# Rows 4p+j in a block, wider load pieces, loads in waves and a first projection by parts in a fused attention and GLU kernel

## The chip, the cores and the metric

The kernel runs on one core of one Trainium2 chip. The time is device microseconds (us) of one execution. A profile's span starts with the first instruction; in these runs the time is about 1.8 us more than the span of the same execution. Comparisons below use the mean time of one kernel's fast runs over that of the other's fast runs of the same rounds, so a ratio is not quite the ratio of the medians quoted beside it. A run more than 1.5% above the fastest of its kernel is called slow and left out of the ratios; for a kernel whose runs scatter the ratio therefore flatters, and the slow runs are named.

## The reference, cut to what matters

```python
x = A_x                                        # 2048 x 512, bf16
h  = x + attention(layernorm(x)) @ wo          # 32 heads of 16, each position sees
                                               # 8 earlier ones, at distances 0, 2, .. 14
h2 = h + ((relu(n @ W_gate)) * (n @ W_up)) @ W_down    # n = layernorm(h), 1376 wide
```

q, k and v come from one 512 x 1536 weight. The attention looks back by position, so k and v must lie in the order of the sequence along a free dimension: the kernel keeps them transposed, features on partitions and positions along the row.

## The kernel before

Four blocks of 512 rows. Each block: statistics on VectorE (DVE), normalised rows, transposes to `xnT`, then twelve groups of four matmuls (q, k, v) whose result ScalarE (ACT) copies out of PSUM, the memory that TensorE (PE) writes to:

```python
x_rows = A_x.rearrange("b (tb p) d -> p (b tb) d", p=P)        # 1 KB pieces
...
for j in range(BPC):
    (nc.scalar if j % 2 else nc.sync).dma_start(x_sm[:, j:j + 1, :], x_rows[:, j:j + 1, :])
for c, q in enumerate((nc.sync, nc.scalar, nc.sync)):          # q, k, v weights
    q.dma_start(w3_sb[c][:], w3_r[:, :, c * D:(c + 1) * D])
for tk in range(1, NCK):                                       # the other blocks of x at once
    nc.sync.dma_start(x_sm[:, tk * BPC:(tk + 1) * BPC, :], x_rows[:, tk * BPC:(tk + 1) * BPC, :])
# ... all other weights ...

def f_mm(lo=0, hi=CS, ...):                                    # one q, k or v group
    for dt in range(NT):
        nc.tensor.matmul(mm.t[:, lo:hi], lhsT=w3_sb[c][:, dt, t:D:NT],
                         rhs=xnT.t[:, dt, lo:hi], start=(dt == 0), stop=(dt == NT - 1))

def f_ev(...):                                                 # its copy out of PSUM
    o = qT.t[:, t, :]            # or kT / vT[:, t, PADL + s0: PADL + s0 + CS]
    nc.scalar.copy(out=o, in_=mm.t[:])
```

The order of instructions on each engine is planned in the program from a table of ranks; the change brings a new table. Matmuls of 128 x 128 `warm` tiles at the start keep TensorE busy while nothing has landed.

The softmax here doesn't subtract the row's maximum and nothing guards it: scores larger than these inputs give would overflow.

## Time and profile before

| | before |
|---|---|
| time, median of the first 3 runs | 203.12 us (202.84 to 203.56) |
| span of the profiled execution | 203.6 us |
| PE busy | 195.4 us |
| ACT busy | 127.7 us |
| first real matmul starts | 10.13 us |

The prediction shows the lines that carry the bound. Two more views matter for what came: the row of the copies of q (those of k and v take the same), with columns count, busy us, mean ns of one, then idle time before and what ended it:

```profile
L519 ACT CAST quad<-bank 128x512 bf16<-128x512 f32 x16 | 9.6, 601 | 7.4 <-PE bank L511 7.4
```

and the table of stretches (start:end, length, busy PE, PEld (PE's weight loads), DVE, ACT, POOL (GpSimd), then granted clock, DMA share, GB/s):

```profile
15.00:20.00 5.00, 5.00 (x38) 3.77 (x36) 4.58 (x12) 3.63 (x9) 0.00 (x0) 0.94 1.03 404
20.00:30.00 10.00, 9.89 (x81) 4.84 (x80) 10.00 (x14) 8.01 (x14) 0.00 (x0) 1.00 0.56 188
30.00:84.00 54.00, 53.56 (x333) 25.64 (x336) 53.45 (x64) 43.75 (x88) 5.56 (x7) 1.00 0.33 64
...
13.70:68.50 54.80, 54.36 (x351) 28.54 (x356) 53.83 (x81) 43.93 (x87) 3.59 (x4) 0.98 0.47 129
```

See the ACT column: ScalarE is a "63%" engine over the whole span, but from 20 to 84 us it is busy 51.8 of 64. The last row runs from the first of the 48 copies to the end of the last: 43.9 of 54.8 us busy, only 10.9 idle.

### The profile page before, as it was taken

What the parts mean: (1) busy time and instruction counts of PE and PEld (TensorE: products, weight loads), DVE (VectorE), ACT (ScalarE), POOL (GpSimd) and SP (SyncE); (2) the same over time, 40 slices, a digit from 0 to 9 for tenths busy, and PEclk for the clock granted to TensorE, in tenths of its full rate; (3) what the DMA queues carried; (4) which work ended last, traced back from release to release, by engine and by line L of the source; (5) the groups of instructions that cost most, each with busy time, mean ns of one, the idle gap of its engine ahead of it and who ended that gap; (6) DMA issues with size and microseconds to landing.
All of it is one profiled execution on the core that took longest, in us unless ns stands there. A gap on an engine that the chain in (4) does not pass through costs nothing.

```text
span 203.6 us, 2957 instructions
## 1 busy us (share of the span) xinstructions
PE 195.4 (96%) x1102; PEld 96.8 (48%) x1123; DVE 155.1 (76%) x246; ACT 127.7 (63%) x253; POOL 12.6 (6%) x26
## 2 busy tenths in 40 slices
PE   8499999999999999999999999999999999999994
PEld 8347545555545334444454444444444445444452
DVE  6549999999999999999999966599996255021314
ACT  3517879986569993797756599703665353576400
POOL 3000000330000002400033000000000000000000
PEclk9859999999999999999999999999999999999999
DMA  5999901698000002980059900400011001100003
GB/s 187 350 379 403 322 19 30 123 203 163 3 0 0 0 3 52 192 168 0 3 103 180 209 31 0 90 13 0 3 41 62 0 0 53 53 0 0 0 3 103
DMA packets 14893, 18.04 MB, mean 89 GB/s; under 512 B 5056, under 2 KB 12192, under 8 KB 14880
## 3 DMA queue, kind: packets, MB, share of 16 engines
q1 hardware_dynamic: 12336, 10.78, 16.4%
q0 software_dynamic: 1728, 6.29, 16.3%
q10 hardware_dynamic: 816, 0.79, 1.1%
q8 instruction: 9, 0.15, 0.3%
q14 instruction: 4, 0.03, 0.0%
HBM read 8.42 MB, written 2.10 MB: 52 GB/s over the span
## 4 chain that ended last, share of the span: by engine, by line
PE 93%; DMA 4%; issue 1%; SPq 0%; DVE 0%
PE bank L736 38%; PE bank L511 22%; PE bank L773 19%; PE bank L698 7%; DMA wq_sb<-in_A_wqkv_dram 4%; PE bank L564 4%; PE bank L465 2%; PE bank L625 1%; PE bank L597 1%; SPq L270 0%; DVE row L784 0%
## 5 line engine op out<-in xcount | busy, mean ns | idle before, releaser
L736 PE MATMUL bank<-quad,wg_sb 128*128 128x512 bf16 (+1 forms) x171 | 42.3, 379 | 0.3
L736 PE MATMUL bank<-quad,wu_sb 128*128 128x512 bf16 (+1 forms) x173 | 42.3, 379 | 0.1
L743 ACT ACTIVATE gr<-bank 128x512 bf16<-128x512 f32 (+1 forms) x44 | 26.0, 604 | 23.7 <-PE bank L736 18.3
L773 PE MATMUL bank<-wd_sb,gT 128*128 128x512 bf16 (+3 forms) x184 | 39.7, 366 | 0.2
L558 DVE TENSOR_TENSOR big<-quad,kT 128x4096 bf16<-128x4096 bf16 x16 | 36.0, 2284 | 0.1
L646 DVE TENSOR_TENSOR big<-big,vT 128x4096 bf16<-128x4096 bf16 x16 | 35.8, 2283 | 0.3 <-ACT big L631 0.3
L740 ACT CAST up_sb<-bank 128x512 bf16<-128x512 f32 (+1 forms) x44 | 25.7, 594 | 12.3 <-PE bank L736 8.5
L756 DVE TENSOR_TENSOR gT<-gr,up_sb 128x1024 bf16<-128x1024 bf16 (+1 forms) x24 | 15.4, 643 | 20.4 <-ACT gr L743 14.1
L773 PEld LDWEIGHTS <-gT 128*128 128x128 bf16 (+1 forms) x187 | 18.0, 98 | 19.3 <-issue 0.4
L736 PEld LDWEIGHTS <-wu_sb 128*128 128x128 bf16 (+1 forms) x176 | 17.3, 100 | 20.7 <-issue 1.3
L736 PEld LDWEIGHTS <-wg_sb 128*128 128x128 bf16 (+1 forms) x176 | 17.3, 100 | 20.6 <-issue 1.1
L511 PE MATMUL bank<-quad,wq_sb 128*128 128x512 bf16 (+1 forms) x70 | 16.9, 382 | 2.5 <-DMA wq_sb<-in_A_wqkv_dram 2.1
L631 ACT CAST big<-bank 128x512 bf16<-128x512 f32 x32 | 17.2, 610 | 1.5 <-PE bank L625 1.3
L511 PE MATMUL bank<-quad,wk_sb 128*128 128x512 bf16 (+1 forms) x70 | 16.8, 373 | 0.1
L678 POOL DMA_DIRECT2D big<-big x12 | 10.7, 894 | 98.3 <-DVE big L646 95.2
L784 DVE TENSOR_TENSOR row<-x_sm,bank 128x512 bf16<-128x512 bf16 (+1 forms) x17 | 10.6, 652 | 7.8 <-PE bank L773 7.8
L649 DVE TENSOR_TENSOR big<-big 128x1024 bf16<-128x1024 bf16 (+2 forms) x24 | 16.4, 727 | 0.0
L709 DVE SCALAR_TENSOR_TENSOR x_sm<-x_sm,bank 128x512 bf16<-128x512 bf16 x16 | 10.9, 685 | 6.8 <-PE bank L698 6.7
L511 PE MATMUL bank<-quad,wv_sb 128*128 128x512 bf16 x62 | 15.4, 379 | 0.1
L698 PE MATMUL bank<-wo_sb,quad 128*128 128x512 bf16 x61 | 14.8, 379 | 0.2
L371 ACT ACTIVATE row<-x_sm,mv 128x512 bf16<-128x512 bf16 x16 | 11.5, 717 | 4.5 <-DVE mv L363 4.4
L519 ACT CAST quad<-bank 128x512 bf16<-128x512 f32 x16 | 9.6, 601 | 7.4 <-PE bank L511 7.4
(65 smaller groups left out, 161.7 us busy)
## 6 DMA issues: line engine op xcount, KB each, us to landing
big<-big POOLq DMA_DIRECT2D x12, 512.0 KB, 5.5
out_dram<-row SPq DMA_DIRECT2D x15, 128.0 KB, 1.7
x_sm<-in_A_x_dram SPq DMA_DIRECT2D x3, 512.0 KB, 11.0
wu_sb<-in_B_W_up_dram SPq DMA_DIRECT2D x1, 1376.0 KB, 10.6
wg_sb<-in_B_W_gate_dram SPq DMA_DIRECT2D x1, 1376.0 KB, 13.9
wd_sb<-in_B_W_down_dram SPq DMA_DIRECT2D x1, 1280.0 KB, 15.7
wq_sb<-in_A_wqkv_dram SPq DMA_DIRECT2D x1, 512.0 KB, 8.4
wk_sb<-in_A_wqkv_dram ACTq DMA_DIRECT2D x1, 512.0 KB, 8.6
```

Of the source, the lines that this page charges most:

```text
L371: nc.scalar.activation(out=xn.t[:], in_=h.t[:] if h else x_sm[:, tk * BPC + j, :], func=ACT.Square, bias=mv.t[:, j, 0:1], scale=1.0, accum ...
L511: nc.tensor.matmul(mm.t[:, lo:hi], lhsT=w3_sb[c][:, dt, t:D:NT], rhs=xnT.t[:, dt, lo:hi], start=(dt == 0), stop=(dt == NT - 1))
L558: V.tensor_tensor(out=pb.t[:].rearrange("p (t w) s -> p t w s", t=2), in0=q4, in1=k4, op=ALU.mult)
L631: nc.scalar.copy(out=ab.t[:, w, :], in_=bc.t[:])
L646: V.tensor_tensor(out=mt.t[:], in0=ab.t[:], in1=v8, op=ALU.mult)
L649: V.tensor_tensor(out=mt.t[:, 0:n, :], in0=mt.t[:, 0:n, :], in1=mt.t[:, n:2 * n, :], op=ALU.add)
L698: nc.tensor.matmul(od.t[:], lhsT=OT.t[:, t, j * P:(j + 1) * P], rhs=wo_sb[:, t, :], start=(t == 0), stop=(t == NT - 1 and tk not in RPE))
L736: nc.tensor.matmul(mm.t[:fs, :], lhsT=w_sb[:, dt, ft * P: ft * P + fs], rhs=hnT.t[:, dt, :], start=(dt == 0), stop=(dt == NT - 1))
L740: nc.scalar.copy(out=ub.t[:fs, i, :], in_=um.t[:fs, :])
L743: nc.scalar.activation(out=gr.t[:fs, i, :], in_=gm.t[:fs, :], func=ACT.Relu)
L756: V.tensor_tensor(out=gt.t[:fs, 0:n, :], in0=gr.t[:fs, 0:n, :], in1=ub.t[:fs, 0:n, :], op=ALU.mult)
L773: nc.tensor.matmul(od.t[:, c0:c1], lhsT=gts[ft].t[:fs, ft % 2, j * P:(j + 1) * P], rhs=wd_sb[:fs, ft, c0:c1], start=(ft == 0), stop=(ft == ...
```

## The change

The intent is to start TensorE earlier: x in 2 to 4 KB pieces and the q and k weights in 2 KB pieces, first what the first projection needs and the rest behind it, and the projection begun on 128 rows as soon as those are ready. Larger pieces of x need partition p to hold the rows 4p to 4p+3 of a block, so that transposed columns come out in the order (j, p) and the copies must put them back in the order of the sequence.

```diff
-    x_rows = A_x.rearrange("b (tb p) d -> p (b tb) d", p=P)
+    x_rows = A_x.rearrange("b (tk p j) d -> p (b tk) j d", p=P, j=BPC)     # output rows likewise
+        for j, q in ((0, nc.sync), (2, nc.scalar)):
+            q.dma_start(x_sm[:, j:j + 2, :], x_rows[:, 0, j:j + 2, :])
+        for dt in range(NT):                          # q and k together, 256 KB a time
+            (nc.scalar if dt % 2 else nc.sync).dma_start(wqk_sb[:, dt:dt + 1, :], w3_r[:, dt:dt + 1, 0:2 * D])
 ...
+        nc.gpsimd.tensor_copy(out=x_sm[0:1, BPC, 0:1], in_=x_sm[0:1, 0, 0:1])      # wait for x block 0
+        nc.sync.dma_start(x_sm[:, BPC:2 * BPC, :], x_rows[:, 1, :, :])
+        nc.gpsimd.tensor_copy(out=wv_sb[0:1, 0, 0:1], in_=wqk_sb[0:1, 3, 0:1])     # wait for q, k
+        nc.sync.dma_start(wv_sb[:], w3_r[:, :, 2 * D:3 * D])
 ...                                                   # then the other blocks and weights
-                nc.scalar.copy(out=o, in_=mm.t[:])
+                nc.scalar.copy(out=o.rearrange("p (c j) -> p j c", j=BPC),
+                               in_=mm.t[:].rearrange("p (j c) -> p j c", j=BPC))
 ...
-    nc.tensor.matmul(od.t[:], lhsT=OT.t[:, t, j * P:(j + 1) * P], rhs=wo_sb[:, t, :], ...)
+    nc.tensor.matmul(od.t[:], lhsT=OT.t[:, t, j:CS:BPC], rhs=wo_sb[:, t, :], ...)
```

Cut: block 0's fourth statistic moves from ScalarE to VectorE, the first four q/k groups go in parts of 128, 128 and 256 rows, filler matmuls follow the first transposes, 44 warm-up matmuls instead of 48, and the table of ranks is new and obeyed strictly.

## The prediction

> **What bounds the kernel now.** I read the page's busy shares and slices first, then the chain of waits in order of time, then the timeline of the first 20 us, then a table of stretches for the granted clock.
>
> ```profile
> PE 195.4 (96%) x1102; PEld 96.8 (48%) x1123; DVE 155.1 (76%) x246; ACT 127.7 (63%) x253; POOL 12.6 (6%) x26
> ...
> PE   8499999999999999999999999999999999999994
> ...
> DVE  6549999999999999999999966599996255021314
> ...
> PEclk9859999999999999999999999999999999999999
> DMA  5999901698000002980059900400011001100003
> ```
>
> See: a slice is 5.09 us. TensorE is full from the fourth slice to the last, so from about 15 us on nothing but the amount of matmul work can move the end. The only soft places are the first three slices, where PE is at 8 and 4 tenths and the granted clock at 8 and 5. DVE is also at 9 from the fourth slice to the twenty-first: a second engine without slack there.
>
> The chain in order of time says which wait ends last in the soft part:
>
> ```profile
> 1.61 0.05 issue
> 1.66 8.42 DMA wq_sb<-in_A_wqkv_dram
> 10.08 0.05 issue
> 10.13 2.32 PE bank L511 x9
> 12.45 0.22 issue
> 12.67 7.27 PE bank L511 x38
> ...
> 200.69 0.42 DVE row L784
> ```
>
> See: one 512 KB weight load, issued at 1.66 us, lands 8.42 us later; the first real matmul waits for it. After it the chain is PE without a break to 200.69. The tail (last add and store, 203.6 - 200.69 = 2.9 us) is untouched by the change.
>
> The timeline shows that the data side was ready before the weights:
>
> ```profile
> 3.48 1.29 DVE L401 BATCH_NORM_STATS2 st<-x_sm 128x6 f32<-128x512 bf16 x2 [0.29 <-DMA x_sm<-in_A_x_dram]
> ...
> 6.21 1.38 DVE L436 TENSOR_SCALAR row<-x_sm,mv,rs 128x512 bf16<-128x512 bf16 x4 [0.20 <-ACT rs L418]
> ...
> 7.51 0.75 DVE L477 COPY quad<-bank 128x512 bf16<-128x512 bf16 x2
> ...
> 10.13 2.32 PE L511 MATMUL bank<-quad,wq_sb 128*128 128x256 bf16 x9 [2.08 <-DMA wq_sb<-in_A_wqkv_dram]
> ```
>
> See: all of the first block's normalised rows are transposed and copied out by about 8.7 us (a ScalarE copy ends then); PE idles 8.05 to 10.13.
>
> The idle time has a second price, the clock:
>
> ```profile
> 8.00:9.00 1.00, 0.05 (x1) 0.00 (x0) 0.26 (x1) 0.61 (x2) 0.00 (x0) 0.90 0.96 310
> 9.00:10.00 1.00, 0.00 (x0) 0.00 (x0) 0.00 (x0) 0.00 (x0) 0.00 (x0) 0.50 1.09 382
> ...
> 14.00:15.00 1.00, 1.00 (x4) 0.40 (x3) 1.00 (x3) 0.35 (x1) 0.00 (x0) 0.50 1.03 401
> 15.00:16.00 1.00, 1.00 (x5) 0.38 (x3) 1.00 (x6) 0.53 (x1) 0.00 (x0) 0.69 1.05 402
> 16.00:17.00 1.00, 1.00 (x7) 0.51 (x5) 1.00 (x2) 0.56 (x3) 0.00 (x0) 1.00 1.01 392
> ```
>
> Columns: stretch, length, busy PE, PEld, DVE, ACT, POOL, then granted clock, DMA share, GB/s. The clock falls to half at about 8.8 (0.90 in that row) and returns at about 15.6. By 16.29 PE did eight 256-column and twelve 512-column matmuls, 8192 columns. At full clock 512 columns take 0.216 us (x38 pieces in the later chain; 1.73 us for x8), so these are 16 x 0.216 = 3.45 us of work that took 16.29 - 10.13 = 6.16. The half clock costs 2.7 us.
>
> **What the Trainium skill says.** "TensorE: Matmul & The Clock Gate", Part 1 (The HAM clock gate): the array's clock is halved by default and after an idle window, restored after a busy one; the window is 3.4 us and free-running. The trace agrees: 8.8 to 15.6 is 6.8 us, two windows. Free-running also means that its phase against the kernel differs by run, which fits the 0.7 us spread of three runs. "DMA: Bandwidth & Descriptors", Issuing engines are not separate DMA queues: loads from several queues interleave on the same 16 engines. Agrees: the DMA share is about 1.0 from 4 to 25 us, so wq waited for its competitors. The same page, Specifications, puts line rate at pieces of 512 B and more; here 1 KB pieces moved at about 350 GB/s (5 to 8 us) and the later mix, with 2.7 and 4 KB pieces among it, at about 400 (14 to 20 us). So I allow larger pieces 10 to 15%, no more. "SBUF — State Buffer", Door 1: lines of 16 bytes, two or more hits in one run at full rate; the new strides of 4 bf16 are 8 bytes. For reads the trace agrees: the strided q/k weight loads take 113 to 118 ns against 98 for contiguous ones, hidden behind 216 ns matmuls. No ScalarE write of this stride is in the trace.
>
> **The change part by part.**
> Larger pieces and waves. Before, x block 0, q, k, v (2 MB) and three more x blocks were all put on the queues by 4 us. Now only x block 0 and q/k (1.57 million bytes) go first, the rest waits behind tiny GpSimd copies that depend on the loads. Bytes start at about 1.9 us (33 GB/s in the row 1:2). At 350 to 380 GB/s they are through at 1.9 + 1.57/0.365 = 6.2, and with up to 1 us from last byte to the waiting engine wq/wk should be usable at about 7.0 instead of 10.08. x block 0 should be there at about 3.7 (3.48 for its first 128 KB row group before). x block 1 follows, 0.52 million bytes more, about 8.5.
> So the weights stop being the bound, and the chain of block 0's layernorm takes over. DVE now takes all four statistics (ScalarE took one), in this static order: two statistics 3.7 to 5.0, two aggregates to 5.3, the third statistic to 6.0, aggregate 6.1, the normalised rows at 6.2, 6.5 and 6.9 (0.33 apart; ScalarE's Ln and Exp of 0.3 and 0.2 before each), the fourth statistic to 7.9, two PSUM copies and an aggregate (0.34 + 0.15 + 0.34) to 8.7, one statistic of block 1 (0.65, if it has landed) to 9.4, the fourth row 9.8. Then a transpose, a ScalarE copy of 0.6: the last 256 rows can be projected from about 10.9 to 11.1.
> Meanwhile PE does 12 transposes, 16 filler matmuls (0.9 us in idle time), then 32 matmuls of 128 columns. Their pace is 56 ns by columns; weight loads of this stride might make it 70 to 113. At 70, 32 x 0.07 = 2.2 us, from 8.5 to 10.7: in time. The first four groups then need 16 matmuls of 256 columns (0.11 each, 1.8 us) and the other four 16 of 512 (3.45 us). The q/k projection of block 0 ends at 11.0 + 5.25 = 16.3, if the clock stays whole. Before, it ended at 19.78, with the same 16 transposes done.
> The rest. Matmul counts after that are the same; before took 203.6 - 19.78 = 183.8 us for it. Moved: strided ScalarE copies of q, k, v (48, about 0.6 us each, I leave them at that), strided loads of wo's stationary operand (hidden), a new fixed order. The first score matmuls need two DVE products of 2.28 us, after the evictions and, in the new order, three statistics of block 2 among them; I get them ready at about 20.9, where PE is ready at 16.3 + 0.9 + 3.45 = 20.7. I add 0.4 us for stalls there and at the second scores.
> Sum: 183.8 + 16.3 + 0.4 = 200.5 us, 1.3% below 203.12. Of the 3.5 us gained at the front 2.7 is clock and the rest earlier weights.
>
> **The rivals.** (1) The clock falls again anyway: warm-up ends at 5.5, the transposes come in three bursts from 6.6, and if the window's phase is bad PE is at half rate for part of the projection. For: before, a stretch that was 63% busy (8.85 to 12.27) did not bring the clock back. Against: fillers cover 7.6 to 8.5 and projection parts follow. It would give 201.5 to 203. (2) LayerNorm faster or weight parts quicker than I think, no stalls: 199 to 199.8. (3) DVE, saturated from 13 to 110 us, becomes the bound: PE's gain is then only DVE's, whose first product moves from 18.84 to about 15; or block 1's x lands late and holds DVE's strict order before the fourth row. 201 to 201.5. (4) Strided ScalarE writes run at half pace: 48 x 0.6 = 29 us more on an engine at 63%, first products 2 us later, 201.5 to 203. No row speaks for it.
>
> **Range and chances.** The middle case gets about 0.55, rivals 1, 3 and 4 together 0.3, rival 2 0.15. Predicted 200.5 us, 199.0 to 202.4 for 8 in 10. Faster by over 2% means below 199.06: 0.12. Within 2%: 0.85. Slower: 0.03; only a badly fitting fixed order could do that.
>
> **What would show it.** Right: wqk's wait gone from the chain or ending near 7 us; the 128-column parts beginning near 8.5, the 256-column ones near 11; clock 1.00 in every row from 8 to 17; the next transposes after the q/k projection near 16.3; ScalarE copies of k still about 600 ns; PE unbroken to the end. Wrong: a wait for wqk beyond 8, a clock of 0.5 after 8, copies near 1 us, PE idle before the score matmuls beyond 1 us.

## The result, and the profile after

| | before | after |
|---|---|---|
| time, median of 6 runs | 203.13 us (202.71 to 204.5) | 223.32 us (222.65 to 224.82) |
| ratio of fast runs | | 1.099 (95%: 1.0945 to 1.1036) |
| ACT busy | 127.7 us | 153.6 us |

10% slower, far outside the range. The page's first lines of the changed kernel (a slice is now 5.6 us):

```profile
PE 202.1 (91%) x1151; PEld 98.4 (44%) x1151; DVE 156.4 (70%) x247; ACT 153.6 (69%) x251; POOL 12.6 (6%) x28
...
PE   7798687957899849999999999999999999999993
...
ACT  2489999997999999668775666693145494157600
...
PEclk9999799999999995999999999999999999999999
```

PE has gaps up to the fifteenth slice, and ACT is at 9 over just this part. The chain of waits, merged in order of time, says the same:

```profile
12.52 0.20 ACT rs L438
12.73 1.20 ACT kT L535
13.93 1.16 ACT quad L535
15.09 1.16 ACT kT L535
16.24 1.16 ACT quad L535
17.40 2.31 ACT kT L535 x2
```

From 12.5 to 83.6 us nearly every link of it is a ScalarE instruction, mostly L535, the copy of q, k or v. Its row, to be held against L519 above:

```profile
L535 ACT CAST quad<-bank 128x512 bf16<-128x512 f32 x16 | 21.8, 1410 | 0.0
```

1410 ns where it was 601, and no idle time before any of them. Those of k and v take 1393 and 1412 ns: together 64.3 us busy for the 48 copies, where they had 28.5. (Neighbouring copies overlap in the records: a copy takes 1.41 us, but the next starts 1.15 us after it. So the sum of these rows is more than the time that they occupy, and the page's total for ACT rose less, from 127.7 to 153.6.) The stretches:

```profile
15.00:20.00 5.00, 5.00 (x37) 3.02 (x36) 3.26 (x3) 5.00 (x6) 0.00 (x0) 1.00 1.02 411
20.00:30.00 10.00, 6.51 (x36) 2.20 (x35) 7.19 (x9) 10.00 (x11) 0.00 (x0) 0.83 0.69 240
30.00:84.00 54.00, 43.08 (x256) 20.31 (x255) 41.21 (x59) 52.66 (x68) 3.59 (x4) 0.99 0.26 49
```

ACT is full, PE and DVE starve, and PE's gaps bring back a half clock now and then (0.83 in the second row). Yet the front is nearly as it was meant to be. The timeline there:

```profile
8.49 1.50 PE L526 MATMUL bank<-quad,wqk_sb 128*128 128x128 bf16 x24
...
9.07 0.70 DVE L421 BATCH_NORM_STATS2 st<-x_sm 128x6 f32<-128x512 bf16 x1 [0.45 <-DMA x_sm<-in_A_x_dram]
...
11.21 5.36 PE L526 MATMUL bank<-quad,wqk_sb 128*128 128x256 bf16 x32 [0.23 <-ACT quad L501]
...
14.82 1.42 ACT L535 CAST kT<-bank 128x512 bf16<-128x512 f32 x1
15.97 1.43 ACT L535 CAST quad<-bank 128x512 bf16<-128x512 f32 x1
```

The parts begin at 8.49, the last 256 rows at 11.21, and the first transposes of the next block follow the projection at 16.41. The copies start 1.15 us apart. One wait was not meant: x block 1 landed at 9.05 us, and DVE, held to its fixed order, waited 0.45 us for it before it could make the fourth row of block 0.

### The profile page after: what moved, and what is told of

The parts are those of the page before. It is cut to its first block, busy times and chain, and to the rows that moved or that the text cites. A ratio compares the mean times of both kernels' runs of the same rounds, so it can differ in the third digit from the quotient of the medians.

```text
span 223.0 us, 3021 instructions
## 1 busy us (share of the span) xinstructions
PE 202.1 (91%) x1151; PEld 98.4 (44%) x1151; DVE 156.4 (70%) x247; ACT 153.6 (69%) x251; POOL 12.6 (6%) x28
## 3 DMA queue, kind: packets, MB, share of 16 engines
q1 hardware_dynamic: 10800, 10.78, 14.7%
## 4 chain that ended last, share of the span: by engine, by line
PE 61%; ACT 30%; DMA 4%; DVE 2%; issue 1%; POOL 0%; ACTq 0%
PE bank L753 36%; PE bank L790 17%; ACT kT L535 8%; ACT quad L535 7%; ACT vT L535 7%; PE bank L715 5%; DMA x_sm<-in_A_x_dram 4%; ACT quad L501 2%; ACT big L648 2%; PE bank L581 1%; ACT row L410 1%; DVE big L575 1%; PE bank L642 1%; ACT ex L597 1%; DVE st L421 1%
## 5 line engine op out<-in xcount | busy, mean ns | idle before, releaser
L753 PE MATMUL bank<-quad,wg_sb 128*128 128x512 bf16 (+1 forms) x176 | 44.5, 391 | 2.8 <-ACT quad L501 2.8
L753 PE MATMUL bank<-quad,wu_sb 128*128 128x512 bf16 (+1 forms) x176 | 43.8, 385 | 0.0
L526 PE MATMUL bank<-quad,wqk_sb 128*128 128x512 bf16 (+2 forms) x160 | 31.7, 342 | 2.1 <-ACT kT L535 1.3
L526 PEld LDWEIGHTS <-wqk_sb 128*128 128x128 bf16 x160 | 15.9, 115 | 15.5 <-issue 6.7
L535 ACT CAST kT<-bank 128x512 bf16<-128x512 f32 x16 | 21.1, 1393 | 1.2 <-DVE big L575 1.2
L535 ACT CAST quad<-bank 128x512 bf16<-128x512 f32 x16 | 21.8, 1410 | 0.0
L535 ACT CAST vT<-bank 128x512 bf16<-128x512 f32 x16 | 21.4, 1412 | 0.0
L526 PE MATMUL bank<-quad,wv_sb 128*128 128x512 bf16 x64 | 17.0, 394 | 2.9 <-ACT vT L535 2.4
L666 DVE TENSOR_TENSOR big<-big 128x1024 bf16<-128x1024 bf16 (+2 forms) x24 | 17.3, 730 | 0.2
L501 ACT COPY quad<-bank 128x1024 bf16<-128x1024 bf16 (+1 forms) x12 | 11.2, 968 | 7.9 <-PE bank L485 7.9
```

Source lines behind the costliest of these rows:

```text
L501: nc.scalar.copy(out=o, in_=i)
L526: nc.tensor.matmul(mm.t[:, lo:hi], lhsT=wv_sb[:, dt, t:D:NT] if c == 2 else wqk_sb[:, dt, c * D + t:(c + 1) * D:NT], rhs=xnT.t[:, dt, lo:h ...
L535: nc.scalar.copy(out=o.rearrange("p (c j) -> p j c", j=BPC), in_=mm.t[:].rearrange("p (j c) -> p j c", j=BPC))
L666: V.tensor_tensor(out=mt.t[:, 0:n, :], in0=mt.t[:, 0:n, :], in1=mt.t[:, n:2 * n, :], op=ALU.add)
L753: nc.tensor.matmul(mm.t[:fs, :], lhsT=w_sb[:, dt, ft * P: ft * P + fs], rhs=hnT.t[:, dt, :], start=(dt == 0), stop=(dt == NT - 1))
```

## The experiments

Theory S: the store with a step of four bf16 elements (8 bytes) makes each copy more than twice as long, and this alone makes ScalarE the bound. Rivals: the new order or the waves (O); other traffic that slows the copies (C); any walk of more than one dimension or with a large step, on either side of the copy (R).

**The four that decide.** The first takes the step away and keeps everything else, the order too (its result is wrong):

```diff
-  nc.scalar.copy(out=o.rearrange("p (c j) -> p j c", j=BPC), in_=mm.t[:].rearrange("p (j c) -> p j c", j=BPC))
+  nc.scalar.copy(out=o, in_=mm.t[:])
```

> The changed kernel with one thing undone: the 48 copies of q, k and v out of PSUM write 512 neighbouring elements instead of every fourth (the result is wrong on purpose, rows land in the wrong order; the instruction order on every engine stays). Theory S (the store with a step of 8 bytes is what makes these copies 1.40 us long and ScalarE the bound from 12.6 to 83.6 us): the copies are back at about 0.60 us, ScalarE's busy time is about 38 us lower, PE is unbroken, and the time is 201 to 203 us. Rival O (the new fixed order or the waves of loads cost the time): the copies shorten but PE still has gaps before 84 us and the time stays above 212. Rival C (the copies are slow because of other traffic at that time): the copies stay above 1 us.

202.5 us median (202.44, 202.53 and 202.47, and a slow run of 207.26), ratio to before 0.992 (0.986 to 0.998). The profile, of 200.6 us span:

```profile
L535 ACT CAST quad<-bank 128x512 bf16<-128x512 f32 x16 | 9.3, 602 | 1.4 <-PE bank L526 1.3
```

```profile
30.00:84.00 54.00, 53.59 (x326) 25.90 (x330) 53.72 (x57) 41.84 (x83) 7.04 (x8) 1.00 0.41 77
```

The copies are short, PE is full again. The whole loss was in that one line; O and C fall. ACT's busy time is 123.4 us, 30.2 below the changed kernel and not the 38 expected: the 38 took the overlap of the copies for work. From the first copy to the end of the last, first the changed kernel, then this one:

```profile
12.50:86.50 74.00, 59.59 (x345) 27.99 (x344) 55.39 (x75) 72.63 (x86) 3.59 (x4) 0.95 0.38 110
...
12.20:65.50 53.30, 52.84 (x339) 27.19 (x344) 52.49 (x75) 42.43 (x86) 3.59 (x4) 1.00 0.52 149
```

The same 86 ScalarE instructions fill 72.6 of 74.0 us, and here 42.4 of 53.3. The step adds 30.2 us of work; idle time takes up 9.5 of it (10.9 us idle become 1.4), and the stretch is 20.7 us longer. With 0.3 us before it and 1.4 after it, that is the 22.4 us between the spans.

The second brings the natural order of rows back and keeps the waves, parts, fillers and order (a correct kernel):

```diff
-  x_rows = A_x.rearrange("b (tk p j) d -> p (b tk) j d", p=P, j=BPC)      # out_rows likewise
+  x_rows = A_x.rearrange("b (tk j p) d -> p (b tk) j d", p=P, j=BPC)
-  nc.scalar.copy(...)  with the step;   lhsT=OT.t[:, t, j:CS:BPC]
+  nc.scalar.copy(out=o, in_=mm.t[:]);   lhsT=OT.t[:, t, j * P:(j + 1) * P]
```

> The changed kernel with rows in their natural order again (x in 1 KB pieces, contiguous copies, contiguous stationary operand of wo), but waves, 2 KB pieces of the q and k weights, the parts of 128 rows, fillers and the new fixed order kept; a correct kernel. Theory S: as the plain-copy run, 201 to 203 us, within 1 us of it, because 2 or 4 KB pieces of x move the first statistic by 0.3 us at most. If the pieces of x matter, it is over 1 us slower than the plain-copy run. Rival O: above 212.

The profiled execution has a span of 201.2 us, 0.6 above the plain-copy one; its 256-column parts begin at 11.39, 0.4 later than there (10.97). The timed runs were 203.03 and 205.28, and two slow ones of 208.29 and 207.34: ratio 1.014 (1.005 to 1.023): unclear, for a reason that came out later. So the pieces of x, the price of which was the whole reordering, are worth at most about half a microsecond in these two profiles, and even that is not shown: the changed kernel, with the large pieces, began at 11.21. What differs is x block 1: it landed at 9.05 us there and at 9.23 here, and DVE waited for it; in the plain-copy profile it landed at 8.32, and DVE did not wait.

The third keeps the rows 4p+j and puts the same reordering on the read side of the copy (correct):

```diff
-  nc.scalar.copy(out=o.rearrange("p (c j) -> p j c", j=BPC), in_=mm.t[:].rearrange("p (j c) -> p j c", j=BPC))
+  nc.scalar.copy(out=o.rearrange("p (c j) -> p c j", j=BPC), in_=mm.t[:].rearrange("p (j c) -> p c j", j=BPC))
```

> The changed kernel with the same reordering done on the other side of the copy: it reads PSUM with a step of 128 fp32 elements and writes 512 neighbouring bf16 elements; a correct kernel. Theory S (the write step is what costs): copies near 0.60 us and 201 to 203 us. Rival R (any walk with a large step or of more than one dimension costs on ScalarE, on either side): copies stay at 1.0 to 1.4 us and the time stays at 212 to 224.

```profile
L535 ACT CAST quad<-bank 128x512 bf16<-128x512 f32 x16 | 9.3, 604 | 1.4 <-PE bank L526 1.3
```

604 ns, span 200.7 us: reading PSUM with a step of 128 elements costs nothing, so R falls. Times 202.53 and 203.81, slow ones 205.82 and 207.54; ratio 0.995 (0.987 to 1.004). With the slow ones the median is 204.81, against 204.33 for the kernel before.

The fourth adds nothing but the step to the kernel before (wrong result; the diff is the first one's reversed):

> The kernel before with only the strided store added to its 48 copies (result wrong on purpose, nothing else of the change). Theory S: each copy takes about 1.40 us instead of 0.60, 48 x 0.80 = 38 us more on ScalarE, and the time rises by 15 to 25 us to 218 to 228, since the kernel before has less than 10 us of ScalarE idle before 84 us. Rival O or C: the copies stay near 0.60 us and the time near 203.

```profile
L519 ACT CAST quad<-bank 128x512 bf16<-128x512 f32 x16 | 21.7, 1413 | 2.4 <-PE bank L511 2.4
```

```profile
30.00:84.00 54.00, 44.35 (x258) 20.75 (x263) 39.01 (x57) 53.97 (x68) 3.60 (x4) 1.00 0.26 49
```

Fast runs of 222.45, 222.53 and 223.68 us, a slow one of 225.84; ratio 1.092 (1.085 to 1.099). The step alone makes the old kernel as slow as the changed one.

**The cost by itself.** A kernel that only repeats single copies of 128 x 512 elements:

```python
for _ in range(4):
    nc.scalar.copy(out=a4[:].rearrange("p (c j) -> p j c", j=4), in_=bank[:].rearrange("p (j c) -> p j c", j=4))
# likewise with steps 1, 2, 8, 16; one run of 512 with step 4; fp32 stores; an SBUF source; VectorE
```

> The disputed cost by itself: a kernel that does nothing but repeat single copies of 128 x 512 elements, four times each, first on ScalarE and then on VectorE, with different walks (it computes nothing of the reference, so the result is wrong on purpose). Theory S (the write step costs on ScalarE, the byte distance being what matters): contiguous bf16 store 0.6 us; step of 4 bf16 (8 bytes) about 1.4 us, in one run of 512 just as in four runs of 128, and from SBUF as from PSUM; stepping on the read side 0.6 us. Rival R (it is the number of runs or the change of walk): the single-run step of 4 stays at 0.6 us, and 16 runs cost more than 2. If the cost is one write per 8 bytes touched instead of several elements joined, steps of 2, 4 and 8 cost alike, and a contiguous fp32 store costs more than the contiguous bf16 one. VectorE: I expect no change from the PSUM source (0.42 to 0.68 us either way).

What the line numbers stand for: ScalarE with bf16 steps 1 (L57), 2 (L59), 4 (L61), 8 (L63) and 16 (L65); a single run of 512 with step 4 (L67); the read side (L69); fp32 with step 2 (L73) and 4 (L75); step 4 from SBUF (L79). VectorE from PSUM with bf16 steps 1 (L83), 4 (L87) and 8 (L89), and from SBUF with steps 1 (L91) and 4 (L93). The profile puts the rows in the order of their busy time:

```profile
L63 ACT CAST a<-bank 128x512 bf16<-128x512 f32 x4 | 9.8, 2444 | 0.1
L89 DVE CAST v<-bank 128x512 bf16<-128x512 f32 x4 | 9.7, 2429 | 0.1
L65 ACT CAST a<-bank 128x512 bf16<-128x512 f32 x4 | 9.5, 2377 | 0.1
L67 ACT CAST one<-bank 128x512 bf16<-128x512 f32 x4 | 5.5, 1368 | 0.1
L79 ACT COPY s<-src 128x512 bf16<-128x512 bf16 x4 | 5.3, 1321 | 0.1
L61 ACT CAST a<-bank 128x512 bf16<-128x512 f32 x4 | 5.2, 1290 | 0.1
L87 DVE CAST v<-bank 128x512 bf16<-128x512 f32 x4 | 5.1, 1286 | 0.1
L75 ACT COPY f<-bank 128x512 f32<-128x512 f32 x4 | 4.2, 1055 | 0.1
L93 DVE COPY w<-src 128x512 bf16<-128x512 bf16 x4 | 2.9, 732 | 0.1
L59 ACT CAST a<-bank 128x512 bf16<-128x512 f32 x4 | 2.9, 727 | 0.1
...
L83 DVE CAST v<-bank 128x512 bf16<-128x512 f32 x4 | 2.8, 692 | 0.1
...
L69 ACT CAST rd<-bank 128x512 bf16<-128x512 f32 x4 | 2.4, 609 | 0.1
L73 ACT COPY f<-bank 128x512 f32<-128x512 f32 x4 | 2.4, 608 | 0.1
...
L57 ACT CAST a<-bank 128x512 bf16<-128x512 f32 x4 | 2.3, 585 | 7.7 <-PE bank L53 7.6
L91 DVE COPY w<-src 128x512 bf16<-128x512 bf16 x4 | 1.4, 343 | 0.1
```

The contiguous store takes 585 ns, the read side 609, fp32 with a step of 2 (also 8 bytes) 608. So on ScalarE the step on the write side is the cost, not the number of runs (one run or four, 1368 or 1290 ns), nor the source (from SBUF 1321). VectorE pays the same from PSUM (692 to 1286), against my guess; from bf16 in SBUF it takes 343 ns without the step and 732 with it, hardly more than its contiguous copy from PSUM, so there the source does matter. It is not the distance in bytes alone either: 8 bytes cost nothing in fp32 and double the time in bf16. It grows with the step up to 16 bytes, and no more from 8 to 16 elements. What in the store path does this, these runs do not say.

**What the front was worth.** The kernel before was profiled once more, unchanged:

> The kernel before once more, unchanged, for a second profile: the first one (203.6 us span) came from an execution that lost its clock from 8.8 to 15.6 us, and timed runs of the same kernel have spans from 200.9 us. Theory: with the window in another phase the half-clock stretch is shorter or absent, the q/k projection of block 0 ends about 17 to 18 us instead of 19.78, and the span is 201 to 202.5; what comes after it takes the same 183.8 us within 0.3. If instead the projection ends near 19.8 again, the spread of the runs has another source.

```profile
9.59 1.93 PE L511 MATMUL bank<-quad,wq_sb 128*128 128x256 bf16 x12 [1.69 <-DMA wq_sb<-in_A_wqkv_dram]
...
17.34 0.40 PE L465 MATMUL bank<-identity,row 128*128 128x128 bf16 x4 [0.61 <-DVE row L436]
```

Span 202.1 us. No half clock, the projection behind it at 17.34 instead of 19.78. What follows took 184.8 us, 1.0 more than in the first profile and not the same within 0.3: DVE made PE wait 0.6 and 0.5 us. The first profile was thus of an execution that had lost 2.7 us to the clock, and an earlier start is worth 1 to 1.5 us against an ordinary one (read-side span 200.7 against 202.1; the fast runs' ratio of 0.995 says 1 us).

Then the waves alone, on the kernel before with its order and rows untouched:

```diff
-  for c, q in enumerate((nc.sync, nc.scalar, nc.sync)): ...      # q, k, v; then all x blocks
+  for c, q in enumerate((nc.sync, nc.scalar)): ...               # q, k; x block 1, v and the rest
+                                                                 # behind two GpSimd copies, as in the change
```

> The kernel before, its order and its row layout untouched, with only the waves of loads: x block 0 and the q and k weights first, the rest behind GpSimd copies. It asks what the sound part of the change is worth. The first projection then waits for the last x copy (8.7 us in the profile) and no longer for the weights (9.6 to 10.1), so it begins at 8.5 to 9 us, the clock is lost less often, and the time is 0.3 to 1.2% below the kernel before: 202 to 203.7 us, with a smaller spread. If the waves delay x block 1 or the v weights into the projection, it is the same or slower.

```profile
9.46 0.77 PE L516 MATMUL bank<-quad,wq_sb 128*128 128x256 bf16 x4 [1.47 <-DMA wq_sb<-in_A_wqkv_dram]
```

A miss: 205.42 us (204.29 to 206.21), ratio 1.005 (1.002 to 1.009): slower than the kernel before, if by little. In the profile x block 2 landed at 16.9 us (14.7 before), and DVE waited 3.2 us for it. In 1 KB pieces the q weights still took 7.8 us from issue to landing, with less traffic beside them. With 2 KB pieces and four loads of 256 KB they took 4.0 to 6.2 us in the changed kernel, and 5.3 to 6.2 in the natural-row one. So the waves alone did not bring the projection forward. What did was not taken apart: the pieces, the number of loads, or their issue, which is 0.5 us earlier in the changed kernel (1.2 instead of 1.7 us), since two loads of x go ahead of them and not four.

**Why the mended kernel scatters.** The read-side kernel ran at 202.5 or at 205 to 207.5 us. I first blamed the clock's window falling over the gap after the warm-up, and lengthened the warm-up from 44 to 52 matmuls, beside the same kernel again:

> The correct kernel with the reordering on the read side, with 52 instead of 44 warm-up matmuls, so that TensorE has at most about 0.3 us of idle time ahead of the first transposes even if all of them run at half clock. Theory W (the runs of 204 to 207.5 us of the read-side kernel are those whose clock window falls badly over the gap between warm-up and transposes): the runs gather at 202 to 203.5, at most one of six over 204.5, and the median is 0.5 to 1.5% below the kernel before. Rival: the spread stays, with about half of the runs over 204, because it comes from the later gaps or from the landing of the loads.

> The read-side kernel once more beside it, for its distribution: 202.5 to 207.5 us, about half of the runs over 204, median 204 to 205, within 1% of the kernel before.

With 52: 202.75 and 205.67, and four slow runs of 207.64 to 208.05: worse, so that theory falls. Again unchanged: 202.43, 203.0, 203.83, 203.85, and slow 205.78 and 207.19. Both profiles fell on slow runs and show where they lose, here the repeated one:

```profile
32.08 5.19 SPq L474 DMA_TRANSPOSE quad<-row  x4
...
41.82 1.03 PE L526 MATMUL bank<-quad,wv_sb 128*128 128x512 bf16 x4 [2.69 <-DMA quad<-row]
```

PE waits 2.69 us for a DMA transpose of block 3. In this profile the slowest of the four landed 5.5 us after its issue, in the fast read-side profile 3.2 (its four began at 29.68). In the slow one the first accumulating DMA (512 KB, issued by GpSimd at 35.87) was on the queues before the last transpose, issued at about 36.1; in the fast one it came at 34.01, after a last transpose at 33.7. But the race is not the first loss. DVE's first statistic of block 2, in the fast read-side profile and then in the repeated one:

```profile
13.68 0.69 DVE L421 BATCH_NORM_STATS2 st<-x_sm 128x6 f32<-128x512 bf16 x1
...
16.11 0.69 DVE L421 BATCH_NORM_STATS2 st<-x_sm 128x6 f32<-128x512 bf16 x1 [2.07 <-DMA x_sm<-in_A_x_dram]
```

x block 2 had landed at 16.1 us instead of 13.1, and of the 4.7 us between the two spans (205.4 and 200.7) 2.4 were behind at this point; with 52 warm-up matmuls the same statistic began at 14.87, 1.2 late. I overlooked this. It speaks for the rival in the expectation of the longer warm-up, the landing of the loads; why that varies was not tested. Nor is the lost race always paid for: in both profiles of the kernel before, too, the last transpose landed 5.4 and 5.5 us after its issue, and PE did not wait for it. Three edits against this race: the transposes of block 3 on TensorE; the first accumulation on VectorE; and the rows of blocks 2 and 3 normalised by turns, so that the transposes leave earlier.

```diff
-  DMAT = (('h',2,0),('h',2,2),('x',3,0),('x',3,2))     # a: transposes of x block 3 on PE
+  DMAT = (('h',2,0),('h',2,2))
-  DACC = tuple((k, t) for k in range(3) for t in range(4))                       # b
+  DACC = tuple((k, t) for k in range(3) for t in range(4) if (k, t) != (0, 0))
+  x2, x3 = (the normalising steps of blocks 2 and 3, by rank)                    # c
+  for o, r in zip([o for pair in zip(x2, x3) for o in pair], sorted(o.prio for o in x2 + x3)):
+      o.prio = r
```

> The read-side kernel with the four DMA transposes of x block 3 replaced by sixteen TensorE transposes and two ScalarE copies at the same place of the order. In the two slow profiles TensorE waited 2.6 to 2.7 us at about 39 to 42 us for the last of these DMA transposes (landed 5.5 us after its issue, behind the 512 KB accumulating DMAs), in the fast one not at all. Theory T (this race makes the runs of 205 to 208 us): they vanish, all six runs lie within 1.5 us of each other, at 202.9 to 204.4 us, since TensorE gains 0.9 us of transposes. Rival (they come from the start, clock or loads): still two or more of six runs over 205 us.

> The read-side kernel with the first of the twelve accumulating DMAs (512 KB each) done as an addition on VectorE (1.22 us), so that the DMA engines are free until about 2 us later, when the last DMA transpose of x block 3 is out. Theory T (the runs of 205 to 208 us are those in which that transpose falls behind the first accumulating DMA): the wait of 2.7 us of TensorE near 39 us is absent in the profile and at most one of six runs is over 205 us; 202.4 to 204 us, VectorE's extra 1.2 us costs 0 to 1 us. Rival (another source): two or more over 205.

> The read-side kernel with VectorE normalising the rows of blocks 2 and 3 by turns instead of block 2 first, so that the DMA transposes of block 3 go out about 1 us earlier and are finished before the accumulating DMAs. Theory T: no wait of TensorE for the DMA transposes, runs within 202.4 to 204 us, save up to 0.7 us that TensorE may wait for the rows of block 2. Rival: two or more of six over 205.

(a) 204.93 to 206.37 us, ratio 1.007: no run above 206.4, all within 1.4 us, but the level is 2 us above what I expected, and four of six are over 205: by the criterion set beforehand this counts for the rival, though with the whole level moved it decides little. (b) 203.21 to 205.97 and a slow 207.29, ratio 1.002: two of six over 205, by its own criterion against the race as the only source, though its profile (a fast run) has no such wait. (c) 203.24, 203.32, 203.38, 203.46, 203.65 and 203.70 us: no slow run, all four transposes landed in 2.4 to 2.5 us, ratio 0.998 (0.9952 to 0.9999). In (c)'s profile x block 2 was not late either (its statistic began at 13.82), so six steady runs do not tell the edit from a run of timely loads. The race is shown in two profiles and gone in (c)'s; that it is the source of the slow runs is not shown. Kernel (c) is correct and the best of the steady versions, 0.2% below the kernel before: an edge, not a gain worth the rewrite.

## Why the prediction was wrong

- **Weights earlier, layernorm of block 0 as the new bound: right.** Predicted 8.5 for the parts, 10.9 to 11.1 for the last 256 rows, 16.3 for the end of the projection; the profile after has 8.49, 11.21 and 16.41. The weights had landed at 7.9, not 7.0, still in time. One link was different: x block 1, forecast for 8.5, landed at 9.05 and held the fourth row for 0.45 us. That is the second half of rival 3, in small.
- **Clock whole at the front: right.** 1.00 to 24 us in the profile after; where it fell later, PE had been starved. (Its first stretch is no reading: the trace's first record of the clock is at 4.2 us, and until then the warm-up matmuls start 107 ns apart, after it 56.)
- **Equal work after it, 0.4 us of stalls: right once the copy is mended.** Predicted span 200.5; the plain-copy, read-side and natural-row kernels have 200.6, 200.7 and 201.2. From the end of the projection the plain-copy kernel took 200.6 - 16.16 = 184.4 us, predicted 184.2. The place of the stalls is not confirmed: its list of waits has none of PE at the score matmuls.
- **"strided ScalarE copies of q, k, v (48, about 0.6 us each, I leave them at that)": this term failed.** They took 1.39 to 1.41 us, one every 1.15 us where they follow each other (0.48 in the plain-copy kernel). With them fell "nothing but the amount of matmul work can move the end": PE waited for ScalarE from 12.5 to 83.6 us. I had read the rule of the Trainium skill ("SBUF — State Buffer", Door 1) as free for 8 bytes, saw that no store of this kind was in the trace, and took silence for no cost. The reads that I called in agreement were weight loads on another engine, and they were 15 to 20% longer than the contiguous ones (113 to 118 ns against 98).
- **Rival 4 named the mechanism and the extra work, and failed at the slack.** Its 29 us more on ScalarE were right: 30.2 by the two rows of the plain-copy run. It set them against "an engine at 63%" and came to 201.5 to 203. But the work falls between the first copy and the last, and there the kernel before has only 10.9 us of idle ScalarE time (43.9 of 54.8 us busy). 29 - 10.9 = 18 us had to lengthen the kernel even if all of that idle time could be used, so about 221 us; 223.3 was measured. This sum was open to me before the run.
- **"Of the 3.5 us gained at the front 2.7 is clock": right for the profiled execution, wrong for the time.** I set that execution's span (203.6, time 205.38) equal to the median time 203.12, which hides a span near 201.3. Against an ordinary run 1 to 1.5 us were to be had. Even the mended kernel would not have been at 200.5 us, but at 202.5 in its best runs.
- **"Larger pieces 10 to 15%, no more", the rest by waves: the waves' part failed**, as the run with waves alone showed; how much the pieces gave stays open. From 2 to 7 us the DMA engines moved 340 and 369 GB/s in the changed and the plain-copy kernel, 289 with waves alone, and 318 and 225 in the two profiles of the kernel before: the executions differ among themselves by more than 15%.
- **A small misreading:** the nines of the DVE line run to the twenty-third slice, not the twenty-first. Nothing in the sum rests on it.

## What to carry to other kernels

A change of layout for the sake of a load is paid where the layout is undone; put the step on the side that is free, measured by one small run of single copies, before building on it. Where a transfer's or a copy's new form is in no trace, its cost is unknown, not zero. And size an extra load by the engine's idle time in the stretch where it falls, not by its share of the span.

## What the Trainium skill lacked or had wrong

- "SBUF — State Buffer", Door 1: it lets bf16 step by up to 8 elements for free, two hits in a line of 16 bytes being enough. For stores the runs differ: ScalarE 585 ns contiguous, 727 at step 2, 1290 at 4, 2444 at 8, 2377 at 16; VectorE from PSUM 692 contiguous, 1286 at 4 and 2429 at 8, but 732 at 4 from bf16 in SBUF. In fp32, steps of 2 and 4 take 608 and 1055 ns. For ScalarE reads of PSUM a step of 128 fp32 elements is free (609 ns).
- "ScalarE: Activation LUTs", What ACT_TABLE_LOAD costs, gives one element per cycle for every function and says nothing of the output's step; a store of every fourth bf16 took 1290 ns for 512 elements, 2.2 times the contiguous one.
- "DMA: Bandwidth & Descriptors", Specifications, puts the minimum for line rate at 512 B; two 512 KB weight loads in 1 KB pieces landed 7.8 and 7.9 us after issue with few competitors, four of 256 KB in 2 KB pieces within 6.2. The cause is not separated from the number of loads, nor from their earlier issue.
- The same page, Rules for kernel authors, says that a transpose next to ordinary DMAs needs nothing. For correctness no run speaks against it; for time, one issued just behind a 512 KB accumulating DMA landed in 5.4 to 5.5 us in five profiles, one issued just ahead of it in 3.2, and others in 2.4 to 2.6.
